# Split transfers, one DMA queue, products on zeros and a new laid-out order in a Fourier filter with a gated convolution

## The chip, the cores and the metric

The kernel runs on one core of one Trainium2 chip. The metric is the device time of one execution in microseconds (us), the median of three executions. The engines are TensorE (PE; its weight loads are listed as PEld), VectorE (DVE), ScalarE (ACT), GpSimd (POOL) and SyncE (SP). DMA transfers are issued by the SP queue (SPq) and, in the first microseconds, by the ACT queue (ACTq) too.

## The reference

Eight sequences of 3200 positions with 256 channels each, in float32:

```python
X = np.fft.rfft(x, axis=1)                      # along the 3200 positions
Yr = Xr @ w_r - Xi @ w_i + b_r
Yi = Xr @ w_i + Xi @ w_r + b_i
Y  = soft_threshold(Yr, 0.01) + 1j * soft_threshold(Yi, 0.01)
y  = np.fft.irfft(Y, n=3200, axis=1)
# then, with xp = y padded by four positions in front:
gate = sigmoid(sum(conv_w[k] * xp[:, k:k + S] for k in range(5)))
out  = (gate * (y @ w_val)) @ w_out
```

## The kernel before, in words

The transform of 3200 = 64 x 50 positions is done in two steps of small matrix products with constant cosine tables (`f1`, `f2` forward, `g1`, `g2` back). For each of the eight sequences b the work comes in pieces:

- `p1` (L523), eight units u: loads 2 x 50 rows of `x` (`load`, L532), multiplies them by `f1` into a PSUM tile of tag `ps_2` (`products`, L549), copies half of it on ACT (`keep`, L564), adds and subtracts on DVE (`fold`, L570) and stores the result to a DRAM tile `a_dram` (`store`, L579).
- `p2` (L603), seven groups d: loads from `a_dram` into `a` (L609), second transform step `s2` (L618), splitting of the result into a high and a low part on ACT and DVE, then for each of 13 units `mixed` (L721): a copy of the bias into a PSUM tile `y_ps` (L727), products with the filter weights (`mix_sum` L747, `mix` L741), one addition on DVE in between (L751), the threshold on ACT and DVE; then the first step back `s1i` (L691) and a store to `z_dram` (L712).
- `positions` (L793), eight blocks k: loads 100 rows from `z_dram` into `zl` (L798), second step back `s2i` (L803), copy into `y_sb`.
- `gated` (L848): the five taps of the convolution (one on ACT, L872, four on DVE, L875), sigmoid, the two matrix products (L845) and the store of `out`.

All of it is put into one list of pieces. `Plan.order` (L136) lays the pieces out in time on a model of the engines: a piece has an engine, a duration, the pieces that it depends on, buffers that it opens, and a number `at`; of the pieces that could start on an engine within a few nanoseconds the one with the lowest `at` is taken. The offsets of `at` for the kinds of pieces are the table `O` (L261). `Plan.run` (L229) then emits the pieces in that order, and each engine executes its own pieces strictly in the order emitted; the waits between engines are semaphores. So the whole kernel is one fixed order per engine, the SP queue included: a transfer whose data isn't ready holds all transfers behind it. The model knows the TensorE clock as a factor of 1.6 until 28 us and 1.2 until 45 us of its own time (`CLOCK`, L241), and the transfer rate as `WIRE` (L242).

Two things are special to the beginning. For the first sequence the first halves of the rows are loaded and stored by SP and the second halves by ACT (`QUEUES`, L521; L544 and L599). TensorE executes 13 products on a zeroed tile of 512 columns (`warm`, L934; each is two instructions in the trace) between the first units. For sequences 0 and 1 the 50 rows of a transfer of `x` or `a_dram` are moved as 48 + 2 rows in two transfers (`ROWS`, L515, `by_rows`, L511); for the others, and for the 100 rows of `zl`, in one.

The weights `w_val` and `w_out` and the taps come as 64-bit floats and are converted by 13 DVE operations each (`from_float64`, L379), whose `at` is `O["later"] + O["spread"] * k`.

Of the kernel before, what the change touches and what calls it, by code (L numbers as in the profile page):

```python
# [10 lines left out]
F32 = mybir.dt.float32  # L11
# [6 lines left out]
B, S, D = 8, 3200, 256  # L18
P = 128
HP = P // 2  # L20
N1, N2 = 64, 50
NH = 2
# [82 lines left out]
class Plan:  # L105
# [30 lines left out]
    def order(self):  # L136
# [41 lines left out]
        while len(done) < len(pieces):  # L178
            best = None
            for e in engines:  # L180
                could = []
                for p in waiting[e]:
                    at = opens(p)
                    if at is not None:
                        could.append((max(free[e], p["ready"], at, wire - BACKLOG if p["kb"] else 0.0), p))
                if not could:
                    continue
                first = min(c[0] for c in could)
                near = [c for c in could if c[0] <= first + SLACK[e]]

                lone = e == "PE" and sum(c[1]["mode"] == "q" for c in near) < 2
                start, p = min(near, key=lambda c: (c[1]["at"] + (0.0 if e != "PE" or c[1]["mode"] != "q" else -O["together"] if mode == "q"
                                                                   else O["hold"] if lone else 0.0), c[0]))
                if best is None or start < best[0]:
                    best = start, p
            assert best is not None, "no piece can begin"
            start, p = best
            e = p["engine"]
            waiting[e].remove(p)
            busy, delay = p["busy"], p["delay"]  # L200
            if e == "PE":
# [9 lines left out]
            p["start"], p["end"] = start, end  # L211
# [17 lines left out]
    def run(self, tc):  # L229
        with tc.manual_schedule():  # L230
            for p in self.order():
                p["fn"]()


# [4 lines left out]
SWITCH = {"rq": 97, "fq": 97, "qr": 100, "qf": 100}  # L239
WEIGHTS = 130  # L240
CLOCK = ((28000, 1.6), (45000, 1.2))  # L241
WIRE = 230  # L242
BACKLOG = 5000
LANDED = 2500

# [5 lines left out]
def act(n, kind="copy"):  # L251
# [6 lines left out]
NW = (NT - 1) * N1 + P  # L258
NG = NT // 2 * P + P
T = float(NU)  # L260
O = {'spread': -43.2582,  # L261
     'hold': 0.1723,
     'together': 1.3472,
     'later': 16.9988,
     'load_x': -1.6525,
     'p1': -3.0866,
     'p1_step': 1.6595,
     'load_a': -5.4475,
     's2': -2.5217,
     's1i': 1.3927,  # L270
     'p3': 3.8457,
     'load_z': -27.5528,
     'y': 14.5177,
     'conv': 12.9924,
     'val': 3.2379,
     'gate': -21.5703,
     'project': 5.6082,
     'late_val': 6.023,
     'late_out': 14.484,
     'turn': -27.2503,  # L280
     'pre': 6.946,
     'mix_sum': -2.1531,
     'p1_1': -2.5925,
     'load_x_1': -0.3328,
     'p1_2': 0.3179,
     'p3_0': -1.1611}
# [9 lines left out]
def fourier_filter_then_gated_conv(ctx: ExitStack, tc: tile.TileContext, x, w_r, w_i, b_r, b_i,  # L296
# [23 lines left out]
    bias_sb = const.tile([P, 3, D], F32, name="bias_sb")  # L320
    cw_sb = const.tile([P, 2, KC], F32, name="cw_sb")
    nlam = const.tile([P, 1], F32, name="nlam")

    y_sb = const.tile([P, 2, (N1 + KC - 1) * N2], F32, name="y_sb")
    mid_sb = const.tile([P, 2, 2, N2], F32, name="mid_sb")

    def buffer(key, tag, shape, dtype=F32):
        pool = ps if tag.startswith("ps_") else dram if tag.endswith("_dram") else sb
        tl[key] = pool.tile(shape, dtype, name=key[0], tag=tag, bufs=SLOTS[tag])
        return tl[key]  # L330

    WORDS = {"xs": 3072, "x": 4 * D, "zl": MB * D, "y_hl": 4 * TB, "g_hl": 4 * TB, "s1": 1024, "tp": 2 * D, "o": 2 * TB, "acc": 2 * TB}
# [186 lines left out]
    STORED = []  # L519
    A_KEYS = {}  # L520
    QUEUES = (("SP", nc.sync), ("ACT", nc.scalar))  # L521

    def p1(b, u, at):  # L523

# [2 lines left out]
        x_tag = ("x" if u < 3 else "zl" if u < 6 else "y_hl") if early else "x"  # L527
        s_tag = ("s1", "g_hl", "xs")[u % 3] if early else "s1"
        p_tag = "ps_2"
        rows = ROWS if b < 2 else ((0, N2),)  # L530

        def load(h):  # L532
            xt = room(kx, x_tag, 4 * D) if h in (0, None) else tl[kx]
            src = x[b].rearrange("(n m) c -> n (m c)", m=N1)
            for g in range(NH) if h is None else (h,):
                eng = QUEUES[g][1] if early else nc.sync
                lo = (N1 - 3 - 4 * u if g else 4 * u) * D
                n = 3 * D if g and u == 0 else 4 * D
                by_rows(eng, xt[half(g), 0:n], src[:, lo:lo + n], rows)
                if n < 4 * D:  # L540
                    by_rows(eng, xt[half(g), n:], src[:, NM * D:(NM + 1) * D], rows)
        if early:
            for h in range(NH):
                add(-100 + u, QUEUES[h][0], 650, lambda h=h: load(h), (), [kx + (h,)], None if h else {kx: x_tag}, kb=200)  # L544
        else:
            add(at + O["load_x"] + O["load_x_1"] * (b == 1), "SP", 700, lambda: load(None), STORED if b == 1 else (),
                [kx + (0,), kx + (1,)], {kx: x_tag}, kb=400, chain="x")

        def products():  # L549
# [26 lines left out]
        add(at + 0.01, "DVE", busy, lambda: fold(0), [kp + (0,), ks + (0,)], [ks + (1,)])  # L576
        add(at + 0.011, "DVE", busy, lambda: fold(1), [kp + (0,)], [ks + (0,)] + ([START[0]] if end else []))

        def store(h):  # L579
            if u == 0 and h in (0, None):  # L580
                buffer(ka, "a_dram", [Q, NM * D])
            dst = tl[ka].rearrange("(h f) mc -> f h mc", h=NH)
            hs = slice(0, NH) if h is None else slice(h, h + 1)
            eng = QUEUES[h][1] if early else nc.sync
            for k in range(2):
                lo = u * 4 * D + k * 512
                n = D if lo == 0 else 0
                by_rows(eng, dst[:, hs, lo + n:lo + 512], st()[k * HP:k * HP + N2, hs, n:], rows)
            if u == 0:
                for g in range(NH) if h is None else (h,):  # L590
                    for r in range(2):
                        eng.dma_start(out=dst[r::2, g, 0:D], in_=st()[r:N2:2, 1 - g if r else g, 0:D])
        for h in range(NH) if early else (None,):
            key = ("a_dram", b, (u, h))
            A_KEYS.setdefault(b, []).append(key)
            if early:
                STORED.append(("stored", 0, (u, h)))
            uses = [ks + (1,)] if h == 0 and u else [ks + (0,)] if h == 1 and u else [ks + (0,), ks + (1,)]
            add(at + 0.02, QUEUES[h][0] if early else "SP", 1300 if early else 1500, lambda h=h: store(h), uses,  # L599
                [key] + ([STORED[-1]] if early else []), {ka: "a_dram"} if u == 0 and not h else None, kb=200 if early else 400)  # L600


    def p2(b, d, at):  # L603
# [189 lines left out]
    def positions(b, k, at):  # L793
# [7 lines left out]
        add(at + O["load_z"], "SP", 400, load, [("z_dram", b, u) for u in range(NU)], [kz + (0,)], {kz: "zl"}, kb=400, chain="zl")  # L801

        def s2i():  # L803
            zt = tl[kz].rearrange("p (m c) -> p m c", m=MB)
# [126 lines left out]
    ki, kw, kv = ("idle", 0), ("warm", 0), ("warm", 1)  # L931
    add(-200, "DVE", 600, lambda: nc.vector.memset(room(ki, "tp", 2 * D), 0.0), (), [ki + (0,)], {ki: "tp"})

    def warm(v, n):  # L934

        for j in range(n):
            key = (kw, kv)[(v + j) % 2]
            pw = tl[key] if key in tl else buffer(key, "ps_y", [P, 2, D])
            nc.tensor.matmul(pw.rearrange("p a d -> p (a d)"), tl[ki][:, 0:P], tl[ki], start=True, stop=True)
# [33 lines left out]
    for b in range(B):  # L973
# [18 lines left out]
    plan.run(tc)  # L992


# ---- launch: one core; outputs as the reference has them
# [22 lines left out]
```

## Time and profile before

| | |
|---|---|
| Median of three executions | 868.22 us (866.73 to 869.12) |
| The profiled execution | 869.32 us, of which the span (first to last instruction) is 867.5 us |
| PE busy / PEld busy | 825.7 us (95%) / 696.1 us (80%) |
| DVE / ACT / POOL busy | 768.2 us (89%) / 612.6 us (71%) / 6.2 us (1%) |
| Mean granted TensorE clock | 0.969 |
| Moved by DMA | 162.25 MB, mean 187 GB/s |

A view of the profile lists instructions by line (L572 is line 572 of the kernel before), with the tiles written and read (`out<-in`), or the busy time of each engine in a stretch of the span, with the granted TensorE clock (PEclk, 1.00 is full), the mean busy share of the 16 DMA engines and the rate. In a timeline the first number is the start and the second the length in us; instructions of a kind that follow each other are put together with their count, and a bracket tells how long the engine sat idle before and what ended that.

### The profile page before, as it was taken

The page shows a single profiled execution, that of the slowest core. Times are in us where ns is not written, and L with a number is a line of the kernel's source. Part 1 is how long each engine was busy: PE and PEld are TensorE (multiplying, and loading weights), DVE is VectorE, ACT ScalarE, POOL GpSimd, SP SyncE. Part 2 cuts the span into 40 slices and gives each one's busy share as a digit, 9 for nine tenths or more (in the row PEclk, how much of TensorE's full clock was granted, in tenths as well). Part 3 has the DMA queues.
Part 4 walks back from the last instruction along what each step waited for, and adds up shares of the span by engine and source line. Part 5 has one row for each costly group of instructions (what it writes and reads, how often), then busy time and mean ns, then how long its engine had stood idle before and what let it go on. Part 6 is the DMA issues. An engine that isn't in the chain of part 4 may idle for free.

```text
span 867.5 us, 23798 instructions
## 1 busy us (share of the span) xinstructions
PE 825.7 (95%) x9814; PEld 696.1 (80%) x9814; DVE 768.2 (89%) x1262; ACT 612.6 (71%) x1030; POOL 6.2 (1%) x11
## 2 busy tenths in 40 slices
PE   6888967999999999999999999999999999999997
PEld 2346755888888888898888898898888999998774
DVE  2526678799999999999999999999999999999996
ACT  1225645788877778787787778877787887776673
POOL 0000000000000000000000000000020000000000
PEclk7578989999999999999999999999999999999999
DMA  6679777768775668557675768557674557324422
GB/s 167 177 175 241 242 190 216 223 204 237 237 225 163 202 197 243 182 167 201 198 235 198 222 195 241 179 170 200 199 237 159 151 150 196 109 84 163 153 70 82
DMA packets 123973, 162.25 MB, mean 187 GB/s; under 512 B 10592, under 2 KB 98298, under 8 KB 123866
## 3 DMA queue, kind: packets, MB, share of 16 engines
q1 hardware_dynamic: 122106, 157.47, 61.3%
q10 hardware_dynamic: 1760, 3.28, 1.5%
q8 instruction: 77, 1.26, 0.6%
q14 instruction: 30, 0.25, 0.1%
HBM read 82.06 MB, written 78.64 MB: 185 GB/s over the span
## 4 chain that ended last, share of the span: by engine, by line
PE 61%; DVE 16%; DMA 11%; ACT 6%; issue 2%; SPq 2%; ACTq 0%; DVEq 0%
PE o_ps L845 12%; PE y_ps L745 11%; PE v_ps L845 10%; PE y_p L811 8%; PE y_ps L749 6%; DVE acc L875 5%; PE z_ps L700 4%; PE s L631 4%; DMA x<-in_x 3%; PE p L553 3%; DMA a<-a_dram 3%; DMA a_dram<-s 3%; DVE s L572 2%; DMA f_sb<-in_f 1%; DVE tp L759 1%
## 5 line engine op out<-in xcount | busy, mean ns | idle before, releaser
L875 DVE SCALAR_TENSOR_TENSOR acc<-y_sb,cw_sb,acc 128x400 f32<-128x400 f32 x512 | 301.5, 627 | 6.1 <-ACT acc L872 4.8
L745 PE MATMUL y_ps<-w_sb,xs 128*128 128x256 f32 x1152 | 156.9, 286 | 11.7 <-DVE y_ps L751 11.7
L745 PEld LDWEIGHTS y_ps<-w_sb,xs 128*128 128x128 f32 x1152 | 144.8, 190 | 22.3 <-DVE y_ps L751 13.7
L845 PE MATMUL o_ps<-gated,wo_sb 128*128 128x400 f32 x744 | 151.4, 349 | 0.7 <-DVE xs L680 0.4
L845 PEld LDWEIGHTS o_ps<-gated,wo_sb 128*128 128x128 f32 x744 | 132.4, 188 | 8.2 <-issue 2.5
L845 PE MATMUL v_ps<-y_hl,wv_sb 128*128 128x400 f32 x648 | 130.0, 347 | 1.4 <-ACT o L912 0.6
L572 DVE TENSOR_TENSOR s<-p,s 128x512 f32<-128x512 f32 (+2 forms) x144 | 89.9, 626 | 37.7 <-ACT s L568 22.6
L845 PEld LDWEIGHTS v_ps<-y_hl,wv_sb 128*128 128x128 f32 x648 | 115.5, 188 | 3.6 <-issue 1.3
L811 PEld LDWEIGHTS y_p<-g_sb,zl 100*64 100x64 f32 x2048 | 89.3, 137 | 26.0 <-issue 4.9
L811 PE MATMUL y_p<-g_sb,zl 100*64 100x100 f32 x2048 | 99.6, 252 | 0.5 <-issue 0.2
L749 PE MATMUL y_ps<-w_sb,xs 128*128 128x256 f32 x576 | 88.5, 292 | 6.0 <-ACT y_ps L727 5.5
L749 PEld LDWEIGHTS y_ps<-w_sb,xs 128*128 128x128 f32 x576 | 78.5, 193 | 16.0 <-ACT y_ps L727 11.3
L757 ACT ACTIVATE tp<-y_ps,nlam 128x512 f32<-128x512 f32 (+1 forms) x104 | 69.5, 672 | 24.3 <-PE y_ps L745 22.2
L872 ACT ACTIVATE acc<-y_sb,cw_sb 128x400 f32<-128x400 f32 x128 | 77.2, 630 | 12.0 <-DVE gated L350 11.9
L553 PE MATMUL p<-x,f_sb 50*64 50x512 f32 x256 | 71.2, 639 | 9.0 <-issue 6.3
L348 ACT CAST gated<-acc 128x800 fp32r<-128x800 f32 x62 | 53.4, 861 | 31.4 <-DVE acc L887 31.2
L759 DVE SCALAR_TENSOR_TENSOR tp<-y_ps,tp 128x512 f32<-128x512 f32 (+1 forms) x104 | 68.6, 663 | 5.8 <-ACT tp L757 5.4
L885 ACT ACTIVATE acc<-acc 128x400 f32<-128x400 f32 x128 | 66.9, 539 | 8.6 <-DVE acc L875 8.3
L560 PE MATMUL p<-x,f_sb 50*64 50x512 f32 x240 | 71.9, 646 | 0.0
L727 ACT COPY y_ps<-bias_sb 128x256 f32<-128x256 f32 x104 | 39.7, 382 | 45.5 <-DVE tp L759 38.5
L348 ACT CAST y_hl<-y_sb 128x800 fp32r<-128x800 f32 x54 | 46.5, 860 | 28.5 <-PE v_ps L845 26.5
L631 PEld LDWEIGHTS s<-f_sb,a 64*64 64x64 f32 x3072 | 52.1, 138 | 15.9 <-issue 6.8
(84 smaller groups left out, 1029.3 us busy)
## 6 DMA issues: line engine op xcount, KB each, us to landing
zl<-z_dram SPq DMA_DIRECT2D x64, 400.0 KB
out<-o SPq DMA_DIRECT2D x126, 200.0 KB
a<-a_dram SPq DMA_DIRECT2D x96, 256.0 KB
z_dram<-z_t SPq DMA_DIRECT2D x48, 512.0 KB
x<-in_x SPq DMA_DIRECT2D x90, 200.0 KB
a_dram<-s SPq DMA_DIRECT2D x90, 200.0 KB
x<-in_x SPq DMA_DIRECT2D x23, 192.0 KB
a_dram<-s SPq DMA_DIRECT2D x15, 192.0 KB
```

The lines of the kernel that those rows point to most:

```text
L348: nc.scalar.copy(out=high(), in_=src())
L553: nc.tensor.matmul(p[k * HP:(k + 1) * HP, 0, :], f1_sb[half(0), 0:HP], xt[half(0), k * 512:(k + 1) * 512], start=True, stop=True)
L560: nc.tensor.matmul(dst, f1_sb[half(1), 0:HP], back[:, 2 * k:2 * k + 2, :], start=True, stop=True)
L572: nc.vector.tensor_tensor(out=st()[lo:hi, h, n], in0=tl[kp][lo:hi, 0, n], in1=st()[lo:hi, 1, n], op=(ALU.add, ALU.subtract)[h])
L631: nc.tensor.matmul(p[e * HP:(e + 1) * HP, h, c, t, :], tl[ka][rows, t, c * P + e * HP:c * P + (e + 1) * HP], f2_sb[rows, (4 * d + t) * N1: ...
L745: nc.tensor.matmul(p[:, 1 - r, :], xm(hx, c, r, i), w_sb[:, m, hw, c, :], start=False, stop=k == 5, skip_group_check=True)
L749: nc.tensor.matmul(tl[ky][:, 0], sm(hx, c, i), w_sb[:, 0, hw, c, :], start=False, stop=k == 5, skip_group_check=True)
L759: add(at + 0.2, "DVE", dve(n * D), lambda: nc.vector.scalar_tensor_tensor(out=tl[kt][:, 0:n], in0=tl[ky][:, 0:n], scalar=LAM, in1=tl[kt][: ...
L811: nc.tensor.matmul(dst[e * HP:(e + 1) * HP], zt[0:Q, m, c * P + e * HP:c * P + (e + 1) * HP], g, start=True, stop=True)
L845: nc.tensor.matmul(p[:, e, 0:TB], w[:, hw, c, e * P:(e + 1) * P], src(hy, c), start=n == 0, stop=n == 5)
L872: nc.scalar.mul(block(acc(c)), y_at(k, c, 0), cw_sb[:, c, 0:1])
L875: nc.vector.scalar_tensor_tensor(out=block(acc(c)), in0=y_at(k, c, j), scalar=cw_sb[:, c, j:j + 1], in1=block(acc(c)), op0=ALU.mult, op1=A ...
```

## The change

1. The first sequence: from unit 2 on, both halves of the rows are loaded by SP (ACT still loads the second halves of units 0 and 1), and all stores to `a_dram` are issued by SP, both halves in one transfer.
2. All transfers of 50 rows (`x`, `a_dram`, all sequences) are split as 48 + 2 rows, and each load of `zl` as 96 + 4 rows.
3. A zeroed tile `zero_sb` is added. After the laying out, `Plan.idle` looks for waits of TensorE between 36 and 200 us of the model's time before a piece that opens a `ps_2` tile, or before the first product into a `y_ps` tile; it puts products of `zero_sb` with itself (128 columns) there, as many as take 0.8 of the wait less 300 ns at 214 ns each. In a new `ps_2` tile they are overwritten by the real products; in `y_ps` they add zero.
4. An ACT copy of one element is put ahead of ACT's first transfers; it brings the loading of ACT's table forward.
5. The model: `WIRE` 230 to 250, duration of an `x` load piece 700 to 1300, of a `zl` load 400 to 700, of the first store 1500 to 3000 ns; all of the offsets `O` but two get new values, so that the order on all engines is laid out anew.

```diff
+    def idle(self, done):
+        opened, first = {}, {}
+        for p in done:
+            for t in p["tiles"]:
+                if t[0] == "y_ps":
+                    if t in p["new"]:
+                        opened[t] = p["end"]
+                    elif p["engine"] == "PE":
+                        first.setdefault(t, p["start"])
+        free = 0.0
+        for p in done:
+            if p["engine"] != "PE":
+                continue
+            at, until = free, p["start"]
+            free = p["start"] + p["busy"]
+            if not FILL[0] < until < FILL[1]:
+                continue
+            places = [(since, t) for t, since in opened.items() if since < until <= first[t]]
+            if "ps_2" in p["new"].values():
+                places.append((p["open"], None))
+            since, t = min(places, key=lambda q: q[0], default=(until, None))
+            n = int(0.8 * (until - max(at, since) - 300) / 214)
+            if n > 1:
+                yield p["n"], t, n
...
-WIRE = 230
+FILL = 36000, 200000
+WIRE = 250
...
-O = {'spread': -43.2582,
-     'hold': 0.1723,
-     'together': 1.3472,
-     'later': 16.9988,
+O = {'spread': -54.683,
+     'hold': 0.7811,
+     'together': 1.4506,
+     'later': 22.3972,
...
-     'load_z': -27.5528,
-     'y': 14.5177,
-     'conv': 12.9924,
+     'load_z': -29.6958,
+     'y': 3.4447,
+     'conv': 28.1693,
...
-     'gate': -21.5703,
+     'gate': -35.0985,
...
+    def zeros(p, n, start):
+        for j in range(n):
+            nc.tensor.matmul(p[:, 0, 0:P], zero_sb, zero_sb, start=start, stop=start, skip_group_check=not start)
...
+        if tag == "ps_2" and ahead:
+            zeros(tl[key], ahead.pop(), True)
...
+    BOTH = 2
...
-        rows = ROWS if b < 2 else ((0, N2),)
+        rows = ROWS
...
-                eng = QUEUES[g][1] if early else nc.sync
+                eng = QUEUES[g][1] if early and u < BOTH else nc.sync
...
-        def store(h):
+        def store():
...
-                by_rows(eng, dst[:, hs, lo + n:lo + 512], st()[k * HP:k * HP + N2, hs, n:], rows)
+                by_rows(nc.sync, dst[:, :, lo + n:lo + 512], st()[k * HP:k * HP + N2, :, n:], rows)
...
-            nc.sync.dma_start(out=zt[0:Q], in_=tl["z_dram", b][:, k * MB * D:(k + 1) * MB * D])
+            by_rows(nc.sync, zt, tl["z_dram", b][:, k * MB * D:(k + 1) * MB * D], ((0, 96), (96, Q)))
...
+    add(-199, "ACT", 1300, lambda: nc.scalar.copy(out=b_sb[HP:HP + 1, 0:1], in_=tl[ki][HP:HP + 1, 0:1]), [ki + (0,)], [("b", 0, 2)])
...
+    add(-199.5, "POOL", 200, lambda: nc.gpsimd.memset(zero_sb, 0.0), (), [("zero", 0, 0)])
```

More of the change, by code (lines that the diff above doesn't have):

```diff
@@ L210, in order @@
             end = start + delay
-            p["start"], p["end"] = start, end
+            p["start"], p["end"], p["open"] = start, end, opens(p)
             done.append(p)
@@ L227, in order, with run @@
         return done
-    def run(self, tc):
+    def idle(self, done):
[22 more added lines that the diff above has]
+                yield p["n"], t, n
+    def run(self, tc, fill=None):
+        done = self.order()
+        more = {n: (t, m) for n, t, m in self.idle(done)} if fill else {}
         with tc.manual_schedule():
-            for p in self.order():
+            for p in done:
+                if p["n"] in more:
+                    fill(*more[p["n"]])
                 p["fn"]()
@@ L260 @@
 T = float(NU)
-O = {'spread': -43.2582,
-     'hold': 0.1723,
-     'together': 1.3472,
-     'later': 16.9988,
[L265 to L271, printed above, removed]
-     'load_z': -27.5528,
-     'y': 14.5177,
-     'conv': 12.9924,
-     'val': 3.2379,
-     'gate': -21.5703,
-     'project': 5.6082,
+O = {'spread': -54.683,
+     'hold': 0.7811,
+     'together': 1.4506,
+     'later': 22.3972,
+     'load_x': -0.7527,
+     'p1': -2.106,
+     'p1_step': 1.6553,
+     'load_a': -11.3736,
+     's2': -1.5394,
+     's1i': -10.692,
+     'p3': 4.2133,
+     'load_z': -29.6958,
+     'y': 3.4447,
+     'conv': 28.1693,
+     'val': 2.4256,
+     'gate': -35.0985,
+     'project': 4.2356,
      'late_val': 6.023,
      'late_out': 14.484,
[L280 to L286, printed above, removed]
+     'turn': -10.0954,
+     'pre': -0.7123,
+     'mix_sum': -1.9016,
+     'p1_1': 3.1662,
+     'load_x_1': -4.8043,
+     'p1_2': 0.0205,
+     'p3_0': -1.4661}
 WARM = 2, 1, 1, 1, 8
@@ L322, in fourier_filter_then_gated_conv @@
     nlam = const.tile([P, 1], F32, name="nlam")
+    zero_sb = const.tile([P, P], F32, name="zero_sb")
     y_sb = const.tile([P, 2, (N1 + KC - 1) * N2], F32, name="y_sb")
     mid_sb = const.tile([P, 2, 2, N2], F32, name="mid_sb")
+    ahead = []
+    def zeros(p, n, start):
+        for j in range(n):
+            nc.tensor.matmul(p[:, 0, 0:P], zero_sb, zero_sb, start=start, stop=start, skip_group_check=not start)
     def buffer(key, tag, shape, dtype=F32):
@@ L543, in p1 @@
             for h in range(NH):
-                add(-100 + u, QUEUES[h][0], 650, lambda h=h: load(h), (), [kx + (h,)], None if h else {kx: x_tag}, kb=200)
+                add(-100 + u, QUEUES[h][0] if u < BOTH else "SP", 650, lambda h=h: load(h), (), [kx + (h,)], None if h else {kx: x_tag}, kb=200)
         else:
-            add(at + O["load_x"] + O["load_x_1"] * (b == 1), "SP", 700, lambda: load(None), STORED if b == 1 else (),
+            add(at + O["load_x"] + O["load_x_1"] * (b == 1), "SP", 1300, lambda: load(None), STORED if b == 1 else (),
                 [kx + (0,), kx + (1,)], {kx: x_tag}, kb=400, chain="x")
@@ L577, in p1 @@
         add(at + 0.011, "DVE", busy, lambda: fold(1), [kp + (0,)], [ks + (0,)] + ([START[0]] if end else []))
-        def store(h):
-            if u == 0 and h in (0, None):
+        def store():
+            if u == 0:
                 buffer(ka, "a_dram", [Q, NM * D])
             dst = tl[ka].rearrange("(h f) mc -> f h mc", h=NH)
-            hs = slice(0, NH) if h is None else slice(h, h + 1)
-            eng = QUEUES[h][1] if early else nc.sync
             for k in range(2):
@@ L587, in store @@
                 n = D if lo == 0 else 0
-                by_rows(eng, dst[:, hs, lo + n:lo + 512], st()[k * HP:k * HP + N2, hs, n:], rows)
+                by_rows(nc.sync, dst[:, :, lo + n:lo + 512], st()[k * HP:k * HP + N2, :, n:], rows)
             if u == 0:
-                for g in range(NH) if h is None else (h,):
+                for g in range(NH):
                     for r in range(2):
[L592 to L600, printed above, removed]
+                        nc.sync.dma_start(out=dst[r::2, g, 0:D], in_=st()[r:N2:2, 1 - g if r else g, 0:D])
+        key = ("a_dram", b, u)
+        A_KEYS.setdefault(b, []).append(key)
+        if early:
+            STORED.append(("stored", 0, u))
+        add(at + 0.02, "SP", 1500 + 1500 * (u == 0), store, [ks + (0,), ks + (1,)],
+            [key] + ([STORED[-1]] if early else []), {ka: "a_dram"} if u == 0 else None, kb=400)
     def p2(b, d, at):
@@ L799, in load @@
             zt = buffer(kz, "zl", [P, MB * D])
-            nc.sync.dma_start(out=zt[0:Q], in_=tl["z_dram", b][:, k * MB * D:(k + 1) * MB * D])
-        add(at + O["load_z"], "SP", 400, load, [("z_dram", b, u) for u in range(NU)], [kz + (0,)], {kz: "zl"}, kb=400, chain="zl")
+            by_rows(nc.sync, zt, tl["z_dram", b][:, k * MB * D:(k + 1) * MB * D], ((0, 96), (96, Q)))
+        add(at + O["load_z"], "SP", 700, load, [("z_dram", b, u) for u in range(NU)], [kz + (0,)], {kz: "zl"}, kb=400, chain="zl")
         def s2i():
@@ L991, in fourier_filter_then_gated_conv, with fill @@
                 gated(b, k - AHEAD, start + (k - AHEAD) * T / NB)
-    plan.run(tc)
+    def fill(t, n):
+        if t is None:
+            ahead.append(n)
+        else:
+            zeros(tl[t], n, False)
+    plan.run(tc, fill)
 _INS = ["x", "w_r", "w_i", "b_r", "b_i", "moe_w_val", "moe_conv_w", "moe_w_out"]
```

## The prediction

> **What bounds the kernel now.** I read the busy times of the page first, then the busy time by stretch, then the timeline of the stretches in which TensorE isn't full. Columns of a stretch: its bounds and length, busy time of PE, PEld, DVE, ACT, POOL with instruction counts, granted clock, DMA share, GB/s.
>
> ```profile
> span 867.5 us, 23798 instructions
> PE 825.7 (95%) x9814; PEld 696.1 (80%) x9814; DVE 768.2 (89%) x1262; ACT 612.6 (71%) x1030; POOL 6.2 (1%) x11
> ...
> 0.00:46.00 46.00, 36.24 (x102) 13.81 (x103) 15.72 (x26) 9.17 (x16) 1.15 (x9) 0.70 0.66 175
> 50.00:110.00 60.00, 51.09 (x699) 38.93 (x700) 34.86 (x57) 30.32 (x51) 0.00 (x0) 0.86 0.85 219
> 110.00:160.00 50.00, 37.30 (x566) 30.42 (x566) 41.09 (x84) 25.98 (x46) 0.00 (x0) 0.93 0.76 197
> 160.00:840.00 680.00, 675.98 (x8358) 597.28 (x8353) 656.07 (x1064) 533.04 (x895) 5.01 (x2) 1.00 0.62 188
> 840.00:867.50 27.50, 21.30 (x80) 14.32 (x78) 19.72 (x32) 12.30 (x20) 0.00 (x0) 0.96 0.28 89
> ```
>
> From 160 to 840 us PE is busy 675.98 of 680 us at full clock, with DMA at 0.62: there the order of PE's own products is the limit, and faster transfers have 4.0 us of idle time to win at most. What can be won lies in the first 160 us, where PE is idle (8.9 us from 50 to 110, 12.7 us from 110 to 160, 21.6 together) and the clock is below 1.00. The profiled execution took 869.32 us, 1.82 more than its span and 1.1 more than the median of 868.22; I take the savings from 869.32 and then those 1.1.
>
> **First sequence by SP.**
>
> ```profile
> 0.75 12.34 ACTq L514 DMA_DIRECT2D x<-in_x  x14
> 1.57 14.20 SPq L514 DMA_DIRECT2D x<-in_x  x16
> 6.05 0.65 PE L553 MATMUL p<-x,f_sb 50*64 50x512 f32 x2 [0.81 <-DMA x<-in_x]
> 13.11 1.28 ACT L566 ACT_TABLE_LOAD   x1 [13.11 <-DMA x<-in_x]
> 14.41 0.59 ACT L566 COPY s<-p 128x512 f32<-128x512 f32 x1
> 26.78 14.88 SPq L514 DMA_DIRECT2D a_dram<-s  x24
> 34.55 0.59 ACT L566 COPY s<-p 128x512 f32<-128x512 f32 x1 [2.35 <-DMA a_dram<-s]
> 42.16 3.86 SPq L514 DMA_DIRECT2D x<-in_x  x10
> 46.06 1.34 SPq L613 DMA_DIRECT2D a<-a_dram  x2
> ...
> DMA packets 4667, 8.03 MB, mean 175 GB/s; under 512 B 1047, under 2 KB 2217, under 8 KB 4664
> 20.00:30.00 10.00, 7.59 (x28) 1.65 (x20) 2.88 (x5) 1.76 (x3) 0.00 (x0) 0.67 0.64 194
> ```
>
> Unit 0's products start at 6.05, but ACT's copy of them at 14.41, because ACT is issuing loads until 13.1; ACT then alternates copies and stores (the eighth copy waits 2.35 us "for a store" and comes at 34.55), the last stores go out by 41.66, and the first load of `a`, which needs every store, at 46.06. With the change ACT issues six loads instead of 18 and no store, so the copies follow the products. What is then late next is the transfers: the packets line, for 0 to 46 us, has 8.03 MB at 175 GB/s. At the 194 GB/s of its best 10 us they take 41.4 us: 4.6 us less. I take **-4.0**. The near end is no gain in rate and a late start: the new ACT copy waits for a first DVE memset and loads the table (1.28), so ACT's first transfer leaves some 2 us later than at 0.75 (an estimate: the 1.28, the memset and the copy), +2 if unit 0 were on the path. It isn't, as 8.4 us lie between its products and its copy now. The far end is the 219 GB/s of the next stretch: 36.7 us, -9.3.
>
> SP takes over loads and stores: 28 loads and 36 stores instead of 16 and 34, 14 more. At the 0.62 us of the 24 stores that is 8.7 us; I cost them at nothing, as those 24 were held up by folds and not by SP, and ten transfers at 42 us took 0.39 us each. If SP was the limit: +8.7 less the 4.6, the upper end, +4.
>
> **The splits.**
>
> ```profile
> L514 SPq DMA_DIRECT2D x<-in_x x152: 231/327/1320, 1.6 to 644.2; - x152
> SPq L914 <- ACT o L912: 144.0, 40, 7.8
> ```
>
> The splits are new for six sequences of `x` and `a_dram` and for all `zl`: 16 + 16 + 8 transfers a sequence, 40, at the median 0.327 us of SP: 13 us a sequence, 80 us in six. They hide in SP's waits, of which the longest kind alone, for the copy of `o`, is 144 us; uncovered they cost up to that 80. The shorter transfers themselves win time where PE waits for them, and after 160 us it has 4.0 us of idle time in all: I take **-1.0** for this stretch, of the new order too; ends -4, all of it, and +4, as much again.
>
> **Products on zeros.**
>
> ```profile
> 50.00:60.00 10.00, 7.46 (x112) 4.50 (x113) 4.95 (x9) 2.49 (x4) 0.00 (x0) 0.65 0.98 187
> 60.00:70.00 10.00, 7.86 (x78) 5.30 (x76) 5.46 (x9) 4.25 (x7) 0.00 (x0) 0.84 0.65 171
> 70.00:80.00 10.00, 9.37 (x115) 8.38 (x116) 5.14 (x9) 4.74 (x8) 0.00 (x0) 0.66 0.96 213
> 110.00:120.00 10.00, 4.62 (x44) 3.15 (x43) 9.48 (x22) 3.45 (x6) 0.00 (x0) 0.89 0.92 230
> 120.00:130.00 10.00, 7.90 (x168) 7.26 (x167) 6.72 (x21) 4.85 (x8) 0.00 (x0) 0.77 0.55 153
> ...
> 39.38 0.34 PEld L939 LDWEIGHTS warm<-idle 128*128 128x128 f32 x1 [0.52 <-issue]
> 40.23 0.34 PEld L939 LDWEIGHTS warm<-idle 128*128 128x128 f32 x1 [0.52 <-issue]
> 45.32 0.19 PEld L939 LDWEIGHTS warm<-idle 128*128 128x128 f32 x1 [0.24 <-issue]
> 45.75 0.19 PEld L939 LDWEIGHTS warm<-idle 128*128 128x128 f32 x1 [0.24 <-issue]
> 58.17 2.93 PE L749 MATMUL y_ps<-w_sb,xs 128*128 128x256 f32 x12
> 70.63 1.65 PE L749 MATMUL y_ps<-w_sb,xs 128*128 128x256 f32 x6 [2.26 <-ACT y_ps L727]
> 119.55 2.93 PE L745 MATMUL y_ps<-w_sb,xs 128*128 128x256 f32 x12 [5.16 <-DVE y_ps L751]
> 151.43 1.75 PE L749 MATMUL y_ps<-w_sb,xs 128*128 128x256 f32 x12 [1.06 <-ACT y_ps L727]
> ```
>
> Products on zeros do raise the clock: in the block of `warm` the loads follow each other by 0.85 us at first and 0.43 at its end. The same twelve products take 2.93 us at half clock and 1.75 at full. Taking the clock as 1.00 or 0.50, it was at half for 7.0 + 3.2 + 6.8 us of the first three stretches and 2.2 + 4.6 of the last two, 23.8 us; PE was busy 0.82 and 0.63 of them, so full clock would save half of that: 7.0 and 2.1 us, if PE set the pace throughout.
>
> ```profile
> 50.38 6.49 DMA f_sb<-in_f
> 66.30 5.81 DMA f_sb<-in_f
> 72.13 5.05 DMA x<-in_x
> ```
>
> From 50 to 80 the chain that ended last lies in these three transfers for 17.4 us of 30, where PE's clock doesn't count: 0.42 x 7.0 = 2.9. Of the other 2.1 I count half, 1.1. That is 4.0, and 0.5 for products that outlast their wait: **-3.5**. Far end -9.1, all of it. The near end is a cost: a product of 512 columns, two loads, took 0.86 us, so one of 128 takes 0.22 at full clock, just what the layout reckons with, and 0.43 at half. If the laid-out waits are the chip's 21.6 us, 0.8 of them are 17.3 us of zeros; half of these behind data already there cost +8.6.
>
> The Trainium skill (TensorE: Matmul & The Clock Gate, Part 1) says that the clock falls after an idle window of about 3.4 us, so that only gaps longer than that cost. The trace disagrees: behind the wait of 2.26 us at 70.63, six products take 1.65 us, half clock. By the page only the wait of 5.16 us would be worth filling, the sum 2.4 us smaller.
>
> **The new order before 160 us.**
>
> ```profile
> 112.22 2.18 DVE L390 TENSOR_SCALAR st<-st 128x512 int32<-128x512 int32 x5
> 119.06 0.43 DVE L751 TENSOR_TENSOR y_ps<-y_ps,bias_sb 128x256 f32<-128x256 f32 x1
> 146.81 1.68 PE L745 MATMUL y_ps<-w_sb,xs 128*128 128x256 f32 x12 [2.78 <-DVE y_ps L751]
> ```
>
> The longest wait is PE's for DVE, which converts `w_val` in one block from 112.22 to 119.03 before the addition at 119.06; the conversion of `w_out` costs 2.78 us in the same way. The new `spread` keeps the block in one piece, only its place moves. The trace can't show where to: the ends are both waits gone, -7.9, and one more like the longest, +5.2. I take the first becoming like the second: 2.78 - 5.16, **-2.0** rounded. The tail (6.2 us of PE idle) I leave as it is, +-2.
>
> **Sum:** -4.0 - 1.0 - 3.5 - 2.0 = -10.5: 869.32 becomes 858.8, and the median 868.22 becomes **857.7**. Its own range, with one or two terms near their ends, is 850 to 864.
>
> **Rivals.**
> 1. *More than that* (0.10): the start reaches its far end, -9.3 instead of -4.0, and the clock stays full, -9.1 instead of -3.5: 847. For it speaks that ACT is out of the way entirely; against it, that transfers share the stretch.
> 2. *The zeros miss* (0.15): the waits of the layout aren't those of the chip, whose PE waits are set by transfers and DVE; the clock falls as before. The sum loses 3.5: 861. This is also where the skill's rule leads, at 860.
> 3. *Given back* (0.14): DVE has 656.07 of 680 us after 160, its work is unchanged, and an earlier start meets an order with more waits in the middle; a gain of 10 is 1.5 us a sequence. Then 868. Against it: DVE's 23.9 us there are more than the gain.
> 4. *Slower, zeros on the path* (0.10): they are emitted ahead of real products and PE is in order, so each that runs behind arrived data delays the chain. Place: 50 to 160 us. Of the 17.3 us worked out above, all behind the data: 868.2 + 17.3 - 7.0 (the other terms) = 878.5. It decides from 7.0 / 17.3 = 0.4 of them on; at half clock in 50 to 80 they take twice their planned time, which speaks for it, the margin of 0.2 and 300 ns against.
> 5. *Slower, the small transfers* (0.04).
>
> ```profile
> DMA packets 100888, 130.37 MB, mean 184 GB/s; under 512 B 6730, under 2 KB 82004, under 8 KB 100798
> ```
>
> After 160 us 130.37 MB move at 184 GB/s in 707.5 us. If the splits held the rate to the 175 GB/s of the beginning, where all was split, that takes 745 us; from 184 down it decides, and at 180 it costs 17 us: 876 with the 9.5 of the other terms. Against it: the beginning was held up by ACT, at a share of 0.66. The Trainium skill (DMA: Bandwidth & Descriptors, Rules for kernel authors) speaks against the change here: it says to merge small transfers, as below 64 KB one pays mostly overhead, and the 2-row pieces are 8 KB; no row of this trace shows a split and an unsplit load alone side by side.
>
> That the change doesn't do what it says has no case of its own but the second.
>
> **The numbers.** Forecast 0.47, the rivals 0.10, 0.15, 0.14, 0.10, 0.04. About 0.3%, 2.6 us, is what a measurement of this kernel can tell from no change. Faster: 0.47 + 0.10 + 0.15 and 0.01 of the fourth rival's mild form, 0.73; same 0.14; slower 0.13. The range takes in the forecast's own and the second and third rival, and half of the first: 847 to 870; the last two stay out with 0.14, and half of the first.
>
> **What would show it.** ACT's first copy near 8 us and the first load of `a` near 42 (first step); clock 1.00 from 50 to 130 with `zero_sb` products in PE's waits (third); the wait for DVE L751 at the first conversion near 3 us (fourth); PE busy over 675 of 680 us in the middle, and 2-row transfers that leave SP waiting (second). The forecast is wrong if the first load of `a` stays at 46, if PE waits for transfers after 160, or if real products start late behind zeros.

## The result and the profile after

| | before | after |
|---|---|---|
| Median of five executions each, run alternately | 867.39 us (866.73 to 869.12) | 862.75 us (861.63 to 864.17) |
| Ratio, with its 95% interval | | 0.9939 (0.9926 to 0.9953) |
| The profiled execution / its span | 869.32 / 867.5 us | 862.75 / 860.8 us |

The kernel is faster by 0.61%, 5.3 us of 867.39 by the ratio (4.6 by the medians). The forecast was 857.7 us, 10.5 less than before: the direction is right, the time lies in the range, and half of the gain isn't there. Where times of different experiments are compared below, each is taken by its own ratio to the kernel before.

First the page's busy times, and the same five stretches as before (bounds and length, busy time of PE, PEld, DVE, ACT, POOL with counts, granted clock, DMA share, GB/s):

```profile
span 860.8 us, 24420 instructions
PE 828.8 (96%) x9938; PEld 709.3 (82%) x9938; DVE 768.7 (89%) x1262; ACT 618.4 (72%) x1031; POOL 4.4 (1%) x12
...
0.00:46.00 46.00, 34.82 (x148) 14.95 (x151) 15.81 (x26) 10.21 (x19) 1.29 (x10) 0.95 0.69 178
50.00:110.00 60.00, 51.25 (x682) 40.35 (x682) 41.80 (x81) 31.80 (x54) 0.00 (x0) 0.90 0.86 223
110.00:160.00 50.00, 48.44 (x707) 41.32 (x705) 40.82 (x72) 32.21 (x57) 0.00 (x0) 1.00 0.85 225
160.00:840.00 680.00, 676.58 (x8303) 600.80 (x8303) 656.86 (x1063) 535.43 (x890) 3.14 (x2) 1.00 0.68 187
840.00:860.80 20.80, 13.69 (x46) 8.01 (x44) 12.68 (x21) 7.22 (x12) 0.00 (x0) 0.99 0.25 80
```

The middle is what it was: PE busy 676.58 of 680 us against 675.98. So nearly all of the span's 6.7 us comes from the first 160 us. PE's busy time there is misleading: from 110 to 160 it rises from 37.30 to 48.44 us, but much of that is products on zeros. I therefore added up in both traces what PE's real products take at full clock, and compared the times at which the same sum is reached. These sums are estimates, good to 1 or 2 us, as the two orders do different products first. By them the new kernel is some 2 us behind at 50 us, some 6 ahead at 80, 1 to 3 ahead at 130, some 6 at 160, and 7 to 9 from 200 us to the end. The lead is won between 50 and 80 us, lost in good part on the way to 130, won back by 160, and carried through the middle.

ACT's copies (start, length, idle time before), SP's queue with its wait ahead of loads of `a` (total, times, longest), and PE's rows up to the first product of `a`:

```profile
8.74 0.58 ACT L607 COPY s<-p 128x512 f32<-128x512 f32 x1 [6.52 <-PE p L601]
27.78 0.58 ACT L607 COPY s<-p 128x512 f32<-128x512 f32 x1 [1.83 <-DMA a_dram<-s]
...
27.23 11.43 SPq L554 DMA_DIRECT2D a_dram<-s  x24
40.76 1.35 SPq L650 DMA_DIRECT2D a<-a_dram  x2
44.14 6.41 SPq L554 DMA_DIRECT2D x<-in_x  x10
SPq L650 <- DMA a_dram<-s: 5.7, 4, 2.0
...
32.93 3.29 PE L363 MATMUL s<-zero_sb 128*128 128x128 f32 x28
44.42 0.48 PE L668 MATMUL s<-f_sb,a 64*64 64x64 f32 x4 [8.20 <-DMA a<-a_dram]
```

ACT's first copy comes at 8.74 instead of 14.41, its eighth at 27.78 instead of 34.55, the last stores leave at 38.66 instead of 41.66, and the first load of `a` at 40.76 instead of 46.06. Something else in these rows has changed: the ten loads of `x` of the second sequence stand behind `a`; before, they stood ahead of it (42.16, 3.86 us).

PE can't use this lead at once. Its 28 zero instructions ahead of `a` end at 36.22, and then it sits idle for 8.20 us until `a` is there, longer than any wait of the kernel before (5.16). The products on `a` then run at half clock.

The products on zeros and the waits of the conversions (PE, then the stretches of 10 us):

```profile
47.61 4.16 PE L363 MATMUL p<-zero_sb 128*128 128x128 f32 x18
51.70 0.65 PE L594 MATMUL p<-x,f_sb 50*64 50x512 f32 x2
52.73 1.68 PE L786 MATMUL y_ps<-w_sb,xs 128*128 128x256 f32 x12
70.60 0.97 PE L786 MATMUL y_ps<-w_sb,xs 128*128 128x256 f32 x6 [1.91 <-ACT y_ps L764]
104.30 2.93 PE L782 MATMUL y_ps<-w_sb,xs 128*128 128x256 f32 x12 [3.99 <-DVE y_ps L788]
116.26 8.20 PE L363 MATMUL y_ps<-zero_sb 128*128 128x128 f32 x72
124.39 1.17 PE L668 MATMUL s<-f_sb,a 64*64 64x64 f32 x64
...
114.79 2.14 DVE L430 TENSOR_SCALAR st<-st 128x512 int32<-128x512 int32 x5
...
40.00:50.00 10.00, 4.77 (x75) 4.50 (x76) 0.74 (x2) 1.51 (x3) 0.00 (x0) 0.57 0.79 178
70.00:80.00 10.00, 9.17 (x124) 7.73 (x124) 4.42 (x9) 4.75 (x9) 0.00 (x0) 0.83 0.89 264
100.00:110.00 10.00, 6.01 (x36) 4.46 (x35) 8.12 (x26) 3.36 (x6) 0.00 (x0) 0.66 0.89 247
120.00:130.00 10.00, 9.46 (x204) 8.41 (x205) 6.64 (x12) 4.53 (x7) 0.00 (x0) 1.00 1.02 247
```

One long wait for a conversion is left, 3.99 us, with half clock behind it (2.93 us for twelve products). The other conversion, which cost 2.78 us, now runs from 114.79 on, beside a wait of PE for `a` that 72 zero instructions fill. The clock drops at 40 to 50 us, a little at 70 to 80, and at 100 to 110; where the 72 ran, it is 1.00.

### The profile page after: what moved, and what is told of

Read it like the earlier page. It is cut to its first block, busy times and chain, and to the rows that moved or that the text cites. A ratio compares the mean times of both kernels' runs of the same rounds, so it can differ in the third digit from the quotient of the medians.

```text
span 860.8 us, 24420 instructions
## 1 busy us (share of the span) xinstructions
PE 828.8 (96%) x9938; PEld 709.3 (82%) x9938; DVE 768.7 (89%) x1262; ACT 618.4 (72%) x1031; POOL 4.4 (1%) x12
## 4 chain that ended last, share of the span: by engine, by line
PE 61%; DVE 20%; DMA 8%; ACT 4%; SPq 2%; issue 2%; DVEq 0%; ACTq 0%
PE y_ps L782 12%; PE o_ps L882 10%; PE v_ps L882 10%; DVE acc L912 9%; PE y_p L848 7%; PE y_ps L786 7%; PE z_ps L737 4%; PE p L594 4%; PE s L668 4%; DMA x<-in_x 3%; DVE acc L924 2%; DVE gated L390 2%; DVE s L613 1%; DMA zl<-z_dram 1%; DVE tp L796 1%
## 5 line engine op out<-in xcount | busy, mean ns | idle before, releaser
L782 PE MATMUL y_ps<-w_sb,xs 128*128 128x256 f32 x1152 | 155.0, 285 | 5.9 <-DVE y_ps L788 5.9
L782 PEld LDWEIGHTS y_ps<-w_sb,xs 128*128 128x128 f32 x1152 | 145.7, 191 | 15.9 <-DVE y_ps L788 7.5
L882 PE MATMUL o_ps<-gated,wo_sb 128*128 128x400 f32 x744 | 154.1, 350 | 0.2 <-DVE xs L717 0.2
L668 PEld LDWEIGHTS s<-f_sb,a 64*64 64x64 f32 x3072 | 54.6, 137 | 29.1 <-issue 16.2
L716 DVE TENSOR_TENSOR sx<-s,sx 128x512 f32<-128x512 f32 x48 | 33.0, 688 | 42.9 <-ACT xs L713 42.5
L668 PE MATMUL s<-f_sb,a 64*64 64x64 f32 x3072 | 57.6, 222 | 11.7 <-DMA a<-a_dram 9.8
```

The source lines that it names most:

```text
L668: nc.tensor.matmul(p[e * HP:(e + 1) * HP, h, c, t, :], tl[ka][rows, t, c * P + e * HP:c * P + (e + 1) * HP], f2_sb[rows, (4 * d + t) * N1: ...
L782: nc.tensor.matmul(p[:, 1 - r, :], xm(hx, c, r, i), w_sb[:, m, hw, c, :], start=False, stop=k == 5, skip_group_check=True)
L882: nc.tensor.matmul(p[:, e, 0:TB], w[:, hw, c, e * P:(e + 1) * P], src(hy, c), start=n == 0, stop=n == 5)
```

## The experiments

Twelve kernels were run, in three groups. The first asks for the parts one by one, from both ends.

**The kernel after without products on zeros.**

```diff
-    plan.run(tc, fill)
+    plan.run(tc)
```

> The changed kernel without its products on zeros, nothing else altered. Theory (the zeros hold the clock): without the 36 products that the changed kernel executes from 116.3 to 124.4 us, that stretch becomes a wait of some 8 us and the clock falls to half for 6.8 us behind it; with some 5 us of PE work there, 2.5 us more: about 865. Rival (the zeros are laid out where the chip's waits aren't): they end just as the next products begin, so part of them runs behind data that is already there, and without them the kernel takes the same or up to 2 us less: 861 to 863.

863.59 us (860.23 to 865.9), ratio 0.9938 (0.9915 to 0.9961): the kernel after has 0.9939. The clock does fall without them; stretches and timeline of this kernel:

```profile
70.00:80.00 10.00, 7.85 (x127) 6.25 (x126) 6.22 (x10) 6.12 (x12) 0.00 (x0) 1.00 0.93 256
120.00:130.00 10.00, 5.05 (x120) 4.05 (x124) 6.05 (x12) 2.97 (x5) 0.00 (x0) 0.55 1.04 254
...
43.28 1.34 SPq L650 DMA_DIRECT2D a<-a_dram  x2
46.66 6.08 SPq L554 DMA_DIRECT2D x<-in_x  x10
52.34 1.97 PE L594 MATMUL p<-x,f_sb 50*64 50x512 f32 x4 [2.03 <-DMA x<-in_x]
55.69 2.93 PE L786 MATMUL y_ps<-w_sb,xs 128*128 128x256 f32 x12
73.53 0.97 PE L786 MATMUL y_ps<-w_sb,xs 128*128 128x256 f32 x6 [1.92 <-ACT y_ps L764]
124.35 0.48 PE L668 MATMUL s<-f_sb,a 64*64 64x64 f32 x4 [6.64 <-DMA a<-a_dram]
```

From 120 to 130 us the clock is 0.55 instead of 1.00, and the product that needs `a` starts at 124.35 instead of 124.39. The zeros hold the clock in a place where a transfer sets the pace (DMA share 1.04): they neither cost nor gain anything there that shows in the time, within some 2 us.

The 18 zero instructions at 47.61 do outlast their wait. With them the products of `x` start 7.6 us after the issue of its loads begins (44.14 to 51.70), without them 5.7 (46.66 to 52.34). The full clock behind them makes up for it: the next products into `y_ps` start 8.6 us after that issue with the zeros and 9.0 without (52.73 and 55.69).

This execution's first load of `a` leaves SP at 43.28, 2.5 us later than in the kernel after, although up to there only PE's zeros differ. So times of the start that are read from one execution each can differ by that much without a cause in the kernel.

**The kernel before with the products on zeros alone** (`idle`, `zeros`, `fill` and `zero_sb` as in the change; 47 products).

```diff
-    plan.run(tc)
+    plan.run(tc, fill)
```

> The kernel before with the products on zeros alone, 47 of them where its own layout has waits. Theory (zeros hold the clock): the half-clock stretches of 53 to 63 and 70 to 77 us get shorter and the kernel gains 2 us, 865.5. Rival (the waits of the layout aren't the chip's): same time within 1 us, 866.5 to 868.5, with the half-clock stretches where they were, or slower where the products outlast their wait.

866.74 us, ratio 0.9981 (0.9967 to 0.9995): 1.6 us less than before, between 0.4 and 2.9. In the old order they gain something, less than the 3.5 of the forecast.

**The kernel before with the first sequence by SP alone** (old offsets, old model).

```diff
-                eng = QUEUES[g][1] if early else nc.sync
+                eng = QUEUES[g][1] if early and u < BOTH else nc.sync
...
-                by_rows(eng, dst[:, hs, lo + n:lo + 512], st()[k * HP:k * HP + N2, hs, n:], rows)
+                by_rows(nc.sync, dst[:, :, lo + n:lo + 512], st()[k * HP:k * HP + N2, :, n:], rows)
```

> The kernel before with the first sequence's transfers by SP alone (ACT loads for units 0 and 1 only, whole stores by SP), its offsets as before, so that the layout is made anew from the new pieces. Theory (ACT held up the first sequence): ACT's last copy of the first sequence near 28 us instead of 34.6, the first load of a near 41 instead of 46, and most of the gain arrives at the end: 863 to 864. Rival (the start is bound by transfers or given back by the waits that the layout puts later): the first load of a is earlier, but the wait for DVE's conversion or for transfers before 160 us grows, 866 to 868.

864.68 us, ratio 0.9956 (0.9939 to 0.9972): 3.8 us less. ACT, SP and the first 46 us in this kernel:

```profile
7.04 0.59 ACT L567 COPY s<-p 128x512 f32<-128x512 f32 x1 [1.56 <-PE p L561]
28.10 0.59 ACT L567 COPY s<-p 128x512 f32<-128x512 f32 x1 [3.54 <-DMA a_dram<-s]
...
23.98 13.20 SPq L514 DMA_DIRECT2D a_dram<-s  x28
37.68 4.18 SPq L514 DMA_DIRECT2D x<-in_x  x10
42.09 1.34 SPq L610 DMA_DIRECT2D a<-a_dram  x2
...
0.00:46.00 46.00, 33.38 (x122) 12.52 (x122) 15.82 (x26) 10.69 (x20) 1.15 (x9) 0.90 0.71 193
```

The stores have left at 37.18, and the ten loads of `x` still stand ahead of `a`, which goes at 42.09: 4.0 us earlier than before, and so is the end of the kernel, within its interval. The transfers of the first 46 us move at 193 GB/s instead of 175, almost the 194 that the prediction had reckoned with.

**The kernel after without splitting the later sequences.**

```diff
-        rows = ROWS
+        rows = ROWS if b < 2 else ((0, N2),)
...
-            by_rows(nc.sync, zt, tl["z_dram", b][:, k * MB * D:(k + 1) * MB * D], ((0, 96), (96, Q)))
+            nc.sync.dma_start(out=zt[0:Q], in_=tl["z_dram", b][:, k * MB * D:(k + 1) * MB * D])
```

> The changed kernel with whole transfers again where before had them (x and a_dram of sequences 2 to 7 in 50 rows, zl in 100), in the same order. Theory (the middle is bound by PE, 676.6 of 680 us busy after and 676.0 before): no change beyond 1 us, 862 to 864, with a lower DMA share of the middle or the same. Rival (the new order leans on the faster transfers): PE waits for zl, x or a appear after 160 us and the time is 866 or more. Second rival (the 256 more transfers cost SP): faster than the changed kernel by 1 us or more.

863.48 us, ratio 0.9938 (0.9922 to 0.9955): the added splits are worth nothing that shows, within some 1.5 us.

The second group asks for the order.

**The kernel after with the old offsets.**

```diff
-O = {'spread': -54.683,
+O = {'spread': -43.2582,
...
-     'turn': -10.0954,
+     'turn': -27.2503,
```

> The changed kernel with the offsets O of before, so that only the new pieces, splits, model numbers and zeros differ from before. Theory (the first sequence by SP is the whole gain, and the new offsets only move waits about): as the kernel before with that part alone, a ratio to before of 0.995 to 0.997, 864 to 866. Rival (the new offsets carry their share): 866.5 or more, that is a ratio over 0.998. Second rival (the new offsets cost): faster than the changed kernel, under 0.993.

876.62 us, ratio 1.0081 (1.0058 to 1.0103): slower than before by 7.0 us, though the transfers, splits and zeros are the new ones.

```profile
110.00:160.00 50.00, 36.45 (x542) 29.97 (x534) 36.08 (x75) 22.63 (x41) 0.00 (x0) 0.86 0.88 236
160.00:840.00 680.00, 670.31 (x8342) 590.30 (x8333) 650.64 (x1053) 530.70 (x888) 2.91 (x2) 1.00 0.66 184
```

PE loses 6.3 us in the middle against the kernel after (670.31 against 676.58), and from 110 to 160 it is busy 36.45 us instead of 48.44, zeros included. Laid out from the new pieces, model numbers and splits, the old offsets give an order that loses more than the start wins. So the rival fits that the new offsets carry their share. Which of the new parts spoils the old order was not taken apart.

**The kernel after with whole transfers of 50 rows everywhere,** from the first sequence on.

```diff
-        rows = ROWS
+        rows = ((0, N2),)
```

> The changed kernel with whole transfers of 50 rows of x and a_dram for every sequence, the first two included (zl stays split), same order. Theory (the transfers bound the first 46 us, and a whole transfer runs on fewer DMA engines): DMA share of the first 40 us lower, the first load of a 3 us or more later than 40.8, 865 to 868. Rival (the number of transfers on SP bounds the first sequence): the first load of a earlier than 40.8 and 861 or less.

862.47 us, ratio 0.9928 (0.9906 to 0.995), not distinguishable from the kernel after. The beginning, which I had expected to suffer:

```profile
0.00:46.00 46.00, 34.94 (x196) 15.75 (x196) 15.72 (x26) 10.41 (x19) 1.30 (x10) 0.85 0.61 185
...
39.07 1.35 SPq L650 DMA_DIRECT2D a<-a_dram  x2
SPq L650 <- DMA a_dram<-s: 11.6, 11, 3.8
```

My theory was right in one half: the share is lower, 0.61 against 0.69, and SP waits longer for whole stores to land, up to 3.8 us against 2.0. But the rate is no lower (185 GB/s against 178), and `a` goes earlier by 1.7 us, not later by 3; two executions with the same order ahead of `a` differed by 2.5 above, so the 1.7 show little. No value of the split shows even there.

**The kernel after without the two large conversions,** two fills in their place, laid out anew.

```diff
+        if n > 100:
+            def fixed():
+                if first:
+                    first()
+                nc.vector.memset(parts()["p"], 0.0)
+                nc.vector.memset(parts()["d"], 0.0625)
+            add(at + O["later"], "DVE", 2 * dve(n, True), fixed, uses, done, new)
+            return
```

> The changed kernel without the conversion of w_val and w_out from 64-bit floats: both are filled with a constant by two DVE memsets instead of 13 operations each, so the output isn't the reference's. Theory (DVE's block before 160 us is what the start now waits for): the PE wait of 4.0 us near 100 us and the half clock behind it go, 857 to 859. Rival (the transfers bound that stretch, and the first load of a of the second sequence comes no earlier): the wait is taken over by the one for that load, now 6.6 us long where it isn't filled with zeros, and the time is 861 to 862.5.

882.87 us, ratio 1.0156 (1.0136 to 1.0176). With less to do it is some 19 us slower than the kernel after, since the planner laid out all the rest differently. It tells nothing about the conversions, and much about the planner.

**The kernel after without zeros, with the conversions' steps not pulled ahead** (`spread` 0).

```diff
-O = {'spread': -54.683,
+O = {'spread': 0.0,
...
-    plan.run(tc, fill)
+    plan.run(tc)
```

> The changed kernel without zeros and with the offset spread at 0 instead of -54.7, so that the 13 steps of a conversion have one priority and other DVE work may come between them. Theory (the block of 13 steps costs, not their sum): no PE wait over 2 us for DVE L788 near the conversions, 860 to 862. Rival (the converted weights are needed soon behind, or the start waits for transfers anyway): the wait moves to the first products with w_val or to the loads of a, 863 or more.

882.83 us, ratio 1.0165 (1.0142 to 1.0187). One offset changes the whole order again; 110 to 160 is where it shows first:

```profile
125.30 1.97 PE L594 MATMUL p<-x,f_sb 50*64 50x512 f32 x4 [5.50 <-DMA x<-in_x]
...
110.00:160.00 50.00, 32.65 (x408) 23.14 (x410) 29.94 (x60) 18.93 (x32) 0.00 (x0) 0.66 0.88 235
```

No wait for DVE L788 over 0.9 us is left there, as the theory had it, but PE now waits 5.50 us for `x`: the rival is right in that the wait moves, though not in where to.

So the third group leaves the layout alone where it can.

**The kernel after with the conversions' steps emptied, the layout unchanged.**

```diff
-                fn()
+                if n < 100:
+                    fn()
+                elif k == 12:
+                    nc.vector.memset(parts()["d"], 0.0625)
```

> The changed kernel in its own laid-out order, with the 13 DVE steps of the conversion of w_val and of w_out left out but for one memset each, so that the output isn't the reference's; the layout still reckons with the steps, so no piece changes its place. Theory (the block of steps costs what its PE wait and the half clock behind it show): 4 us of wait and some 3 us of half clock go, 856 to 858.5. Rival (the load of a for the second sequence ends next and as late as before): the PE wait of 4 us goes, that for the load grows by as much, 861 to 863.

859.59 us, ratio 0.9896 (0.9874 to 0.9919), 3.7 us below the kernel after: between what the two theories expected.

```profile
101.43 1.68 PE L785 MATMUL y_ps<-w_sb,xs 128*128 128x256 f32 x12 [0.53 <-DVE y_ps L791]
111.65 8.20 PE L363 MATMUL y_ps<-zero_sb 128*128 128x128 f32 x72
...
50.00:110.00 60.00, 53.42 (x719) 42.72 (x722) 40.57 (x79) 33.57 (x58) 0.00 (x0) 0.96 0.85 230
```

The wait of 3.99 us is 0.53, the twelve products take 1.68 instead of 2.93, the clock from 50 to 110 is 0.96 instead of 0.90, and everything behind comes 4.6 us earlier (111.65 against 116.26). This block of DVE's is what remains of the old longest wait.

**The new order with the old queues:** ACT loads and stores the second halves of the first sequence again; order and zeros are those of the kernel after on PE, DVE and POOL.

```diff
-                eng = QUEUES[g][1] if early and u < BOTH else nc.sync
+                eng = QUEUES[g][1] if early else nc.sync
...
-                by_rows(nc.sync, dst[:, :, lo + n:lo + 512], st()[k * HP:k * HP + N2, :, n:], rows)
+                for h in range(NH) if early else (None,):
+                    hs = slice(0, NH) if h is None else slice(h, h + 1)
+                    by_rows(QUEUES[h or 0][1], dst[:, hs, lo + n:lo + 512], st()[k * HP:k * HP + N2, hs, n:], rows)
```

> The changed kernel in its own order on PE, DVE and POOL, but with the first sequence's second halves loaded and stored by the ACT queue again, as before had it (the transfers stand in ACT's order where the changed kernel has them on SP). Theory (taking these transfers off ACT is the gain): ACT's copies of the first sequence wait for its transfers again, the first load of a comes 3 us or more later than 40.8 and the time is 866 to 869. Rival (the order is the gain, not the queue): the first load of a within 1.5 us of 40.8 and 862 to 864.

863.65 us, ratio 0.9947 (0.9928 to 0.9966), 4.6 us below before.

```profile
15.93 0.58 ACT L607 COPY s<-p 128x512 f32<-128x512 f32 x1 [13.70 <-DMA x<-in_x]
36.98 0.58 ACT L607 COPY s<-p 128x512 f32<-128x512 f32 x1 [4.31 <-DMA a_dram<-s]
...
25.93 13.96 SPq L554 DMA_DIRECT2D a_dram<-s  x24
41.38 1.42 SPq L652 DMA_DIRECT2D a<-a_dram  x2
44.79 6.41 SPq L554 DMA_DIRECT2D x<-in_x  x10
...
37.53 9.51 PE L980 MATMUL warm<-idle 128*128 128x512 f32 x16
46.88 3.29 PE L363 MATMUL s<-zero_sb 128*128 128x128 f32 x28
50.10 1.16 PE L670 MATMUL s<-f_sb,a 64*64 64x64 f32 x64
```

My theory falls here. ACT's copies are as late as before the change (15.93, 36.98), and `a` still goes at 41.38, since the ten loads of `x` stand behind it. But that isn't how this kernel gains either: PE still has its products of `warm` and 28 zero instructions to do, and its first product on `a` starts at 50.10, as late as before (49.95). By the same sum of real products as above it is some 4 us behind the kernel before at 50 us and some 5 to 6 ahead at 80. What in the new order wins this is not shown.

**The kernel after without the early ACT copy** (this changes the order in about a dozen places).

```diff
-    add(-199, "ACT", 1300, lambda: nc.scalar.copy(out=b_sb[HP:HP + 1, 0:1], in_=tl[ki][HP:HP + 1, 0:1]), [ki + (0,)], [("b", 0, 2)])
```

> The changed kernel without the early ACT copy that brings the table load forward; the layout changes in a dozen places on DVE and ACT. Theory (the table load of 1.3 us then stands before ACT's first copy at 8.7 us, and ACT has time there): 862 to 864. Rival (ACT's first copies end the first sequence, so the load costs in full): 1.3 us more, 864 to 865.

861.43 us, ratio 0.9911 (0.9883 to 0.994): no loss.

**The kernel after without zeros and without any split:** whole 50-row transfers, whole `zl` loads.

```diff
-        rows = ROWS
+        rows = ((0, N2),)
...
-    plan.run(tc, fill)
+    plan.run(tc)
```

> The changed kernel without zeros and with whole transfers everywhere, in its own order: of the change, the first sequence by SP, the early table load and the new offsets are left. Theory (these are all that counts): 861.5 to 863.5, a ratio to before of 0.992 to 0.995. Rival (zeros and splits each hide the lack of the other): 865 or more.

859.87 us (858.78 to 866.34), ratio 0.9913 (0.9882 to 0.9944): at least as fast as the kernel after, and simpler. Whether it beats it stays open, since the intervals overlap.

## Why the prediction was right, and where it was wrong

The direction was right. The range, 847 to 870, says less: it also takes in no gain at all, 868. Of the sum, the first term came true on its own, and the other three, -6.5 together, brought 1.5 beyond it.

**The start, -4.0: right on its own, not as a term of the sum.** ACT's first copy "near 8 us" came at 8.74, the first load of `a` "near 42" at 40.76, and this part alone gives -3.8 (b_sp), by the reason given: the rate of the first 46 us rises from 175 to 193 GB/s, for the 194 reckoned with. The price of SP's 14 further transfers, put at nothing, was nothing that shows. In the kernel after the rate is only 178 GB/s, and `a` goes early also because the new order has the ten loads of `x` behind it. Before, two things stood ahead of `a` on SP's queue: the late stores (until 41.66) and these ten loads (3.86 us). With the first gone `a` goes at 42.09, with the second gone at 41.38, with both gone at 40.76, as SP then waits for the stores to land, from 38.66 on; differences under 2.5 us between these single executions show little. I had quoted the row of the ten loads without asking whether the new order would keep them there. And the rest of the change, with ACT as busy as before, gives -4.6 (a_both), so the gain of the start doesn't add to what the order gives.

**The splits and the middle, -1.0: right in sign, without the splits' help.** PE's idle time in the middle fell by 0.6 us. Without the splits the time is the same (a_nosplit, a_whole), so that the 80 us of SP's work, an estimate of the prediction, are hidden, as costed.

**The clock, -3.5: the step that failed.** The mechanism is there in part: zeros hold the clock at 1.00 where they stand (0.55 without). The step converted half clock into time by fractions, 0.42 and a half, of what PE would save; measured, it is nothing in the new order (a_nozeros) and 1.6 us in the old one (b_zeros). Three causes show. At the long fill, PE's next real product waits for `a`, and it starts at the same time either way (124.39 and 124.35); what full clock saves behind it isn't visible in the time. At the first `a`, the layout's wait isn't the chip's: the 28 zero instructions end at 36.22, 8.20 us before `a` is there, and the clock is 0.57 from 40 to 50; the next 18 run at that clock, 4.16 us instead of some 2, and outlast their wait. And the wait for DVE L788, 3.99 us with half clock behind it, has no zeros: `idle` looks only ahead of the first product into a `y_ps` tile, and this wait lies before the second twelve (L782). With the conversions' steps emptied, this wait and its half clock are gone and the kernel is 3.7 us faster (a_noconv_same). The sign "clock 1.00 from 50 to 130" was therefore half wrong: 0.90 from 50 to 110, 1.00 from 110 to 160. The Trainium skill (TensorE: Matmul & The Clock Gate, Part 1) has the clock fall after an idle window of about 3.4 us. That is no better borne out after than before: around the wait of 1.91 us at 70.60 the clock of 70 to 80 us is 0.83. But the length of a wait alone doesn't decide here: around one of 1.92 us at 73.53 in a_nozeros it is 1.00.

**The order, -2.0.** The first conversion's wait went from 5.16 to 3.99, not to 2.78; the second, costed as unchanged, went from 2.78 to nothing visible, as its block now lies beside PE's wait for `a`. Together 4 us of waits are gone, but new waits for `a` have come: 8.20 us at the start, and one of 6.6 us that the zeros fill (a_nozeros). Beyond the start alone, all the rest of the change brings 1.5 us (0.9956 to 0.9939, intervals that overlap). What the prediction missed is the other side of the offsets: with the new pieces and model the old ones give 876.62, so a refit was needed to keep any gain.

**The rivals.** The second, zeros that miss, is nearest: 861 against 862.75. It spoke of waits in other places than planned, and two such waits were indeed missed, that of 8.20 us and that of 3.99; at the long fill the place was met and worth nothing. That the time lies so near to 861 is luck in part, since the other three terms weren't met as summed either. The third, given back in the middle, didn't happen: the lead at 160 us, some 6, is 6.7 at the end. The fourth happens on a small scale at 47.61, but a_nozeros shows no loss in the time; the fifth is excluded by a_nosplit. Forecast and rivals also shared a fault: the terms were added as if independent, whereas the queue alone gives 3.8 us, the rest without the queue 4.6, and both together 5.3.

**What stays open:** why the two overlap, and what in the new order wins its 4.6 us between 50 and 80 us, when its first product on `a` comes no earlier (a_both). Not tried: zeros ahead of the second products into a `y_ps` tile, the place that the runs point to.

## What to carry to other kernels

Two edits that each win time at the same place need not add up: list everything that stands ahead of a transfer on its queue, what it waits for when all of that is gone, and when the engine that needs it is free. Here half clock cost time only where PE's products, not a transfer, released the next step; a fill of zeros elsewhere showed up as busy time and clock, not in the end. In a kernel whose order is laid out by a planner, test one part with the order held fixed: laid out anew, the same work took up to 20 us more here, four times the gain in question.

## What the runs showed of the hardware that was not expected

- Transfers of 50 rows as 48 + 2 kept the DMA engines busier without moving more: a share of 0.69 and 178 GB/s in the first 46 us, against 0.61 and 185 GB/s for whole ones.
- 72 zero instructions of 128 columns took 8.20 us (0.114 each) and held the clock at 1.00; 18 of them at 47.61 took 4.16 (0.23 each), at half clock, behind PE's wait of 8.20 us for `a`.
- Two waits of PE of the same length, 1.91 us at 70.60 in the kernel after and 1.92 at 73.53 without zeros, had a granted clock of 0.83 and 1.00 in the stretch of 70 to 80 us.
- Loading ACT's table early or at the first copy made no difference in the time (0.9911 without the early copy, 0.9939 with it, the intervals overlapping).
